# Zeroing the score banks on ScalarE, adding the residual on TensorE, and ending VectorE on its branch, in a decode step of an attention and MLP block

## The chip, the core and the metric

The kernel runs on one core of a Trainium2 chip. The metric is the device time of one execution in microseconds (us), lower is better. A core has five engines with queues of their own: TensorE (PE; its weight loads are listed as PEld), VectorE (DVE), ScalarE (ACT), GpSimd (POOL) and SyncE (SP), which here issues the DMA transfers. PSUM has eight banks of 128 x 512 fp32; matrix products land there.

## The reference

One token (`x`, 512 wide) goes through a grouped-query attention over a cache of 16,384 positions and then through an MLP, each with a layer norm ahead and a residual behind. There are 32 query heads, 8 key/value heads and a head width of 128.

```python
x = A_x
h = x + _A_ref(_layernorm(x), k_cache, v_cache, wq, wo)
h2 = h + _B_ref(_layernorm(h), w1, w2, w3, w4)

def _A_ref(x, k_cache, v_cache, wq, wo):
    q = (x @ wq)
    ...
    scores = einsum("bhqd,bhkd->bhqk", q, k) * (Dh ** -0.5)
    o = einsum("bhqk,bhkd->bhqd", softmax(scores), v)
    return o.reshape(B, Sq, Hq * Dh) @ wo

def _B_ref(x, w1, w2, w3, w4):
    ...
    x1 = x + hs
    h2 = _gelu(_layernorm(x1) @ w3) @ w4
    return x1 + h2
```

With a single position (S = 1) the shifted groups in `_B_ref` hold nothing but padding, so `hs` is zero, `x1 = x`, and `w1` and `w2` are never read. What must be read is 79.17 MB, nearly all of it the two caches.

## The kernel before

**Program.** The kernel describes operations to a small planner, `Program`. Each operation names its engine, what it reads and writes (`r`, `w`) and the PSUM banks it uses (`bank`). The planner derives semaphore waits from these. Operations of one engine run in the order of the text. `_run` writes an engine's operations out straight. `_vector` and `_tensor` write VectorE's and TensorE's, with branches: TensorE's program is a loop over the four pairs of key/value heads, with inner loops, and a straight part behind it. An operation whose function is `None` (L805 for VectorE, L808 for TensorE) marks the place of a conditional branch that is never taken and that carries a prefetch hint, placed at the program's start (L146, L223). VectorE's branch (L154) waits for the second piece of `w4` and has two instructions behind it: a wait for GpSimd's `xsum`, and the last addition (L815).

**Loads.** SyncE issues all large loads from `load` (L467), in program order: `wq`, then for each pair two halves of keys (4 MB each, into the two halves of `kb`) and the values (8 MB, into `vb`), then `wo` in three pieces, `w3` in two and `w4` in four, over the space of the keys. A load of keys waits until VectorE has transposed the half that it overwrites (L644); a load of values waits until TensorE has used the values before. The last pair's values come in two halves.

**A pair.** VectorE copies the pair's queries from `qb` into `qn` (L729). For each half `y`, VectorE transposes the keys piece by piece into `kt` (L644). TensorE first zeroes score bank `y` by a product of a zero column with itself (L655, part "clear"), since the 32 products of the half (L661, eight pieces of four, part "key") all add to that bank (`start=False`). In `_tensor` the clear has its own block, `pe_half`, with a wait of its own. Then comes the softmax: a maximum over both banks (L671), small steps, the exponential on ScalarE (L682), and two transposes of `p_sb` (L686). Meanwhile TensorE runs nine products that nobody reads (`unread`, L507, a loop of one product). Then come the sums, the values (L697, 64 products), and the gathering of the pair's output (L713 to L721).

**After the pairs.** ScalarE loads the table of the gelu (L746). `o_b` is multiplied by `wo` in 32 products (L766), of which the first 16 use the first piece, 12 the second and 4 the third; between the first 16 and the rest stand four unread products (L765). Then come the layer norm's sums (L521 to L533, L774), `hc` on ScalarE (L780), `w3` (L786, 16 products into bank 0), the inverse roots on VectorE and GpSimd (L540 to L569), `xs` and `xsum` on GpSimd (L793, L795; `xsum` is the sum of the two residuals), gelu (L798), a transpose to `hcol` (L802), and `w4`: 14 blocks `m` of four products (L810) that add in `n_ps`. Blocks 0 to 3 use w4's first piece, 4 to 8 its second, 9 to 12 its third, 13 its fourth. At the end VectorE adds `n_ps` and `xsum` into `fin` (L815), and SyncE writes four rows of `fin`, 256 bytes each, to the output (L817) and waits until they have arrived (L819).

Of the kernel before, what the change touches and what calls it, by code (L numbers as in the profile page):

```python
# [9 lines left out]
ALU = mybir.AluOpType  # L10
ACTF = mybir.ActivationFunctionType
# [13 lines left out]
class Program:  # L25
# [132 lines left out]
    def _tensor(self):  # L158
# [7 lines left out]
        last = pairs - 1  # L166

        def places(kind, *rest):
            return sorted(a for a in at if a[0] == kind and a[1:1 + len(rest)] == rest)
# [6 lines left out]
        def most(o):  # L176
            return max((d.val for d in o.deps if d.eng == "DVE" and not d.dma), default=0)
# [7 lines left out]
        for o in loop:  # L185
            if least(o) > have:
                have = least(o)
                if o.at[1] == last:
                    waits[o.at] = have
        first = waits["clear", last, 0, 0]  # L190
        keys = {("clear", last, 0, 0): first}
        keys |= {("key", last, y, c, 0): first + 1 + pieces * y + c for y in range(2) for c in range(pieces)}
        rest = {(a[0], a[-1]): v for a, v in waits.items() if a[0] in ("middle", "rest")}
        assert all(a in keys or (a[0], a[-1]) in rest for a in waits)
        waits |= keys | {("clear", last, 0, 0): first + 1}
        final = max(waits.values())


        have = 0
        for o in loop:  # L200
            a = o.at
            v = waits.get((a[0], last, *a[2:]))
            if v is not None:
                have = v + (a[1] - last) * step
                assert most(o) >= have - (a[0] == "clear")
            assert least(o) <= have


# [46 lines left out]

        nc.switch_bb("pe_queried", parent=None)
        eng.reg_add(rq, rq, width - 2 * width * pairs)
        eng.br_lt(rq, 2 * width - self.c0, "pe_query", "pe_half")

        nc.switch_bb("pe_half", parent=None)  # L260
        self.y = eng.snap(ry, donate=True, min_val=0, max_val=512)
        eng.wait_ge(vector, r)
        for a in places("clear", 1, 0):
            self._issue(eng, at[a])
        eng.br("pe_piece")

        nc.switch_bb("pe_piece", parent=None)
        self.q = eng.snap(rq, donate=True, min_val=0, max_val=QPAD)
        self.k = eng.snap(rk, donate=True, min_val=0, max_val=KP * (pieces - 1))
        eng.wait_ge(vector, r)  # L270
# [11 lines left out]
        eng.reg_add(ry, ry, 512)  # L282
        eng.reg_add(rq, rq, 4 * pieces)
        eng.reg_add(rk, rk, -KP * pieces)
        eng.br_lt(ry, 2 * 512, "pe_half", "pe_middle")

        nc.switch_bb("pe_middle", parent=None)
        now, again = first + 1 + 2 * pieces, 0
# [31 lines left out]
        eng.reg_add(r, r, first + 1 - (final - step))  # L320
        eng.reg_add(ry, ry, -2 * 512)
        eng.reg_add(rq, rq, -again)
        eng.br_lt(rl, v0 - 1 + parts * pairs, "pe_half", "pe_after")

        nc.switch_bb("pe_after", parent=None)
        seen[id(vector)] = final
# [14 lines left out]
            done = more + 1  # L341
        self._run(eng, ops[done:on], seen)

        eng.br_lt(rl, 0, "pe_half", "pe_on").branch_hint(hint)
        nc.switch_bb("pe_on", parent=None)
        self._run(eng, ops[on + 1:], seen)

# [28 lines left out]
def bass_sequential_preLN__gqa_block_cached__mixer_s_mlp__decode_kernel(  # L376
# [13 lines left out]
    with ExitStack() as ctx:  # L390
# [101 lines left out]
        def dve(fn, r=(), w=(), bank=()):  # L492
            return P.op("DVE", fn, r, w, bank)

        def act(fn, r=(), w=(), bank=()):
            return P.op("ACT", fn, r, w, bank)
# [4 lines left out]
        def pe(fn, r=(), w=(), bank=(), also=()):  # L501

            return P.op("PE", fn, r, w, bank, also=also)
# [6 lines left out]
        def piece(cuts, m):  # L510
            return [lo <= m < hi for lo, hi in cuts].index(True)

        def copies(col, n):

            return col.to_broadcast([col.shape[0], n])
# [132 lines left out]
            part = kt[:, :].rearrange("p (x f) -> p x f", x=2)[:, :, bass.ds(at, KP)]  # L648
            return part.rearrange("p x (l b s e) -> p b e x l s", l=8, b=2, s=32, e=2)[:, n // 2, n % 2, :, :, :]

        none = qn[:, 0, 0:1]

        def scores(j, y):
            P.part("clear", j, y)
            pe(lambda e: e.matmul(row[:, bass.ds(P.y, 512)], copies(none, 128), copies(none, 512),  # L655
                                  start=True, stop=False, skip_group_check=True),
               r=["qn"], w=[("s", y)], bank=[("s", y)])
            for c in range(8):
                P.part("key", j, y, c)
                for n in range(4):  # L660
                    pe(lambda e, n=n: e.matmul(  # L661
                        row[:, bass.ds(P.y, 512)], qn[:, n, bass.ds(P.q, 128)], key_piece(P.k, n),
                        start=False, stop=(n == 3), skip_group_check=True),
                       r=["qn", ("kt", c)], w=[("s", y)], bank=[("s", y)])

        both = dict(bank=[("s", 0), ("s", 1)])

        def softmax(j):

            s_all = s_ps[:, :, :].rearrange("p y f -> p (y f)")  # L670
            dve(lambda e: e.tensor_reduce(mx[:, :], s_all, AX.X, ALU.max), r=[("s", 0), ("s", 1)], w=["mx"], **both)  # L671
            dve(lambda e: e.tensor_scalar(mxd[:, :], ident_f[:, :], mx[:, 0:1], None, ALU.mult),  # L672
                r=["mx", "ident_f"], w=["mxd"])
            pe(lambda e: e.matmul(m_ps[:, 0:128], mean4[:, :], mxd[:, :], start=True, stop=True),  # L674
               r=["mxd", "mean4"], w=["m"], bank=["mn"])
            dve(lambda e: e.tensor_reduce(nm[:, :, :], m_ps[:, 0:128].rearrange("p (g n h) -> p g h n", g=2, h=REP),
                                          AX.X, ALU.min), r=["m"], w=["nm"], bank=["mn"])
            dve(lambda e: e.scalar_tensor_tensor(nmh[:, :], nm[:, :, :].rearrange("p g h -> p (g h)"),  # L678
                                                 32 * D * SCALE, maskgh[:, :, :].rearrange("p g h -> p (g h)"),
                                                 ALU.mult, ALU.mult, accum_out=bias[:, :]),  # L680
                r=["nm", "maskgh"], w=["nmh", "bias"])
            act(lambda e: e.activation(p_sb[:, :], s_all, ACTF.Exp, bias=bias[:, 0:1], scale=float(SCALE),  # L682
                                       accum_out=acc[:, :]),
                r=[("s", 0), ("s", 1), "bias"], w=["p", "acc"], **both)
            for g in range(2):
                dve(lambda e, g=g: e.transpose(pt[64 * g:64 * g + 64, :, :, g, :], p_sb[64 * g:64 * g + 64, :]),  # L686
                    r=["p"], w=["pt"])
# [37 lines left out]

        load_values(0)
        for j in range(PAIRS):
            P.part("query", j)
            dve(lambda e, j=j: e.tensor_copy(qn[:, :, :], qb[:, :, j, :]), r=["qb"], w=["qn"])  # L729
            for y in range(2):  # L730
                P.part("half", j, y)
                transpose_keys(y, (0, 2, 4, 6) if j < PAIRS - 1 else range(8) if y else (0, 1, 2, 4, 6))
                scores(j, y)
                if j < PAIRS - 1:
                    load_keys(j + 1, y)
            P.part("middle", j)
            softmax(j)
            unread(9)
            sums(j)
            values(j)  # L740
            P.part("rest", j)
            gather(j)
            if j < PAIRS - 1:
                load_values(j + 1)
# [16 lines left out]

        for r_ in range(32):
            q = r_ % 4
            if r_ == WO[1][0]:
                unread(4)  # L765
            pe(lambda e, r_=r_, q=q: e.matmul(O_ps[0][32 * q:32 * q + 32, :], copies(o_b[:, r_:r_ + 1], 32),  # L766
                                              wo_sb[:, r_ * D:(r_ + 1) * D], start=(r_ < 4), stop=(r_ >= 28)),
               r=["o_b"] + [("r", 0, n) for n in (piece(WO, r_),) if n], w=[("O", 0)], bank=[("O", 0)])
# [15 lines left out]
        for k in range(NCH):  # L784
            for q in range(4):
                pe(lambda e, k=k, q=q: e.matmul(s_ps[32 * q:32 * q + 32, 0, 0:FQ], hc[:, k, :],  # L786
                                                w3_sb[:, k, q * FQ:(q + 1) * FQ], start=(k == 0), stop=(k == NCH - 1)),
                   r=["hc"] + [("r", 1, n) for n in (piece(W3, k),) if n], w=[("s", 0)], bank=[("s", 0)])
        variances(1, (0, 1))
        seeds(1, (0, 1))  # L790
        inverse_root(1, 1, dve, act)
# [14 lines left out]
        for m in range(NHC):  # L806
            if m == W4[1][0]:
                pe(None)  # L808
            for o in range(4):
                pe(lambda e, m=m, o=o: e.matmul(  # L810
                    n_ps[32 * o:32 * o + 32, 0:128], hcol[:, m, :], w4_sb[:, m, o * 128:(o + 1) * 128],
                    start=(m == 0), stop=(m == NHC - 1),
                    skip_group_check=True),
                   r=[("hcol", 2 * m // NHC)] + [("r", 1, len(W3) + n) for n in (piece(W4, m),) if n], w=["n"], bank=["mn"])
        dve(lambda e: e.tensor_tensor(fin[:, :], n_ps[:, 0:128], xsum[:, :], ALU.add), r=["n", "xsum"], w=["fin"],  # L815
            bank=["mn"])
        P.op("SP", lambda e: e.dma_start(out[0, 0:1, :].rearrange("o (q j) -> (o q) j", q=4), fin[0:128:32, :]),  # L817
             r=["fin"], w=["out"], dma="out")
        P.op("SP", lambda e: e.nop(), r=["out"])  # L819
# [31 lines left out]
```

## Time and profile before

| | |
|---|---|
| median of three runs | 192.34 us (192.22 to 192.51) |
| time of the profiled execution | 192.24 us |
| its span, first to last instruction | 190.3 us |
| busy in the span: PE, DVE, ACT, POOL | 125.7, 117.9, 9.2, 7.4 us |
| moved by DMA | 79.20 MB, mean 416 GB/s |
| granted TensorE clock, mean | 0.86 |
| zeroing products, L655 | 8, together 4.0 us |
| exponentials on 128 x 1024, L682 | 4, 1.11 us each |
| last pair's second half of the values released by its load | 168.19 us |
| last addition, L815 | 187.32 us, 0.29 long |

All times inside a profile count from the start of the span. The span and the device time differ by what lies around the span, here 1.9 us. A line such as "L810 PE MATMUL banks<-kb,hcol" names the source line, the engine, the operation, what it writes and what it reads. In brackets stands how long the engine had been idle before it and what released it.

### The profile page before, as it was taken

The numbers are of one execution on the slowest core, as the hardware profiler recorded it, in microseconds if no ns is written. First come the engines' busy times: TensorE is split into PE (matmuls) and PEld (weight loads), VectorE is DVE, ScalarE is ACT, GpSimd is POOL, SyncE is SP. The second block draws the span as 40 slices with busy tenths as digits, with TensorE's granted clock in tenths as the row PEclk, the third lists the DMA queues.
The fourth block names the chain that finished last, engine by engine and source line by source line (L and its number), as shares of the span: only waits on it lengthen the run. The fifth ranks groups of instructions, "written<-read, shape, count | busy, mean of one in ns | idle before, by whom it ended". The sixth has DMA issues, their size and how long they took to land.

```text
span 190.3 us, 2315 instructions
## 1 busy us (share of the span) xinstructions
PE 125.7 (66%) x733; PEld 48.5 (25%) x733; DVE 117.9 (62%) x152; ACT 9.2 (5%) x16; POOL 7.4 (4%) x16
## 2 busy tenths in 40 slices
PE   0119709997770599964944989658359996865552
PEld 0103303442230233321311433213113332321131
DVE  6740799995523989845049989450479895522270
ACT  3000000000200000011000000020000000500030
POOL 7100000000000000000000000000000000000050
PEclk9999995899999579998585899996858999799755
DMA  6999999999999999997999999889999999999991
GB/s 221 441 441 441 441 441 441 441 441 441 399 413 420 420 551 441 441 441 331 441 441 441 551 399 399 386 379 420 441 441 441 441 441 441 441 386 395 423 408 46
DMA packets 3330, 79.20 MB, mean 416 GB/s; under 512 B 384, under 2 KB 512, under 8 KB 1280
## 3 DMA queue, kind: packets, MB, share of 16 engines
q1 hardware_dynamic: 3320, 79.17, 97.1%
q8 instruction: 1, 0.02, 0.0%
q14 instruction: 1, 0.01, 0.0%
q10 hardware_dynamic: 8, 0.00, 0.0%
HBM read 79.17 MB, written 0.00 MB: 416 GB/s over the span
## 4 chain that ended last, share of the span: by engine, by line
DMA 66%; DVE 15%; PE 14%; issue 2%; SPq 1%; DVEq 0%
DMA kb<-in_A_k_cache_dram 45%; DMA kb<-in_B_w_dram 14%; DVE kt L644 14%; PE banks L661 9%; DMA vb<-in_A_wq_dram 6%; PE banks L621 5%; SPq L467 1%; DVE qcol L628 1%; PE banks L655 1%; DVE qb L635 0%; PE banks L810 0%; DVE xn L612 0%; DVE fin L815 0%; SPq L139 0%; DVEq L139 0%
## 5 line engine op out<-in xcount | busy, mean ns | idle before, releaser
L644 DVE STREAM_TRANSPOSE kt<-kb 128x2048 int32<-128x2048 int32 (+1 forms) x37 | 71.3, 1989 | 6.9 <-DMA kb<-in_A_k_cache_dram 5.3
L661 PE MATMUL banks<-kt,qn 128*128 x256 | 68.9, 416 | 0.9 <-DVE kt L644 0.2
L661 PEld LDWEIGHTS banks<-kt,qn 128*128 x256 | 26.5, 104 | 41.4 <-issue 23.8
L697 PE MATMUL banks<-vb,pt 128*32 128x512 bf16 x256 | 19.2, 463 | 3.5 <-POOLq L482 3.0
L655 PE MATMUL banks<-qn 128*128 128x512 bf16 x8 | 4.0, 495 | 19.6 <-DVE kt L644 19.5
L713 DVE TENSOR_SCALAR od<-banks,rowc 128x128 f32<-128x128 f32 x4 | 1.4, 351 | 21.9 <-PE banks L697 21.9
L507 PE MATMUL banks<-qb 128*128 128x512 bf16 x40 | 14.3, 434 | 0.3
L686 DVE STREAM_TRANSPOSE pt<-p_sb 64x1024 bf16<-64x1024 bf16 x8 | 9.9, 1240 | 5.4 <-ACT p_sb L682 5.3
L621 PE MATMUL banks<-vb,xn 128*128 x32 | 9.0, 451 | 6.1 <-DVE xn L612 6.1
L682 ACT ACTIVATE p_sb<-banks,bias 128x1024 bf16<-128x1024 f32 x4 | 4.5, 1114 | 155.4 <-DVE nmh L678 155.4
L697 PEld LDWEIGHTS banks<-vb,pt 128*32 128x32 bf16 x256 | 7.6, 114 | 13.3 <-issue 5.6
L671 DVE TENSOR_REDUCE mx<-banks 128x1 f32<-128x1024 f32 x4 | 4.9, 1225 | 8.1 <-PE banks L661 8.1
L628 DVE STREAM_TRANSPOSE qcol<-banks 64x1024 f32<-64x1024 f32 x4 | 4.8, 1228 | 7.2 <-PE banks L621 7.2
L563 POOL TENSOR_SCALAR st<-st 128x1 f32<-128x1 f32 x1 | 0.2, 243 | 176.5 <-DVE st L543 176.5
L507 PEld LDWEIGHTS banks<-qb 128*128 128x128 bf16 x40 | 4.2, 107 | 9.3 <-issue 8.8
L655 PEld LDWEIGHTS banks<-qn 128*128 128x128 bf16 x8 | 0.8, 100 | 22.5 <-issue 22.3
L621 PEld LDWEIGHTS banks<-vb,xn 128*128 128x128 bf16 x32 | 3.6, 113 | 11.1 <-issue 8.6
L674 PE MATMUL banks<-mxd,mean 128*128 128x128 f32 x8 | 2.0, 332 | 6.6 <-DVE mxd L672 6.6
L719 PE MATMUL banks<-od,zo 128*32 128x128 f32 x8 | 1.6, 285 | 6.5 <-DVE od L716 6.5
L716 DVE SCALAR_TENSOR_TENSOR od<-banks,rowc,od 128x128 f32<-128x128 f32 x12 | 4.2, 351 | 0.4
L766 PE MATMUL banks<-kb,o_b 128*32 128x512 bf16 x32 | 2.5, 409 | 3.0 <-DMA kb<-in_A_wo_dram 1.8
L588 PE MATMUL banks<-x,quarter 4*128 4x128 bf16 x1 | 0.3, 285 | 6.0 <-DVE quarter L586 6.0
(77 smaller groups left out, 48.5 us busy)
## 6 DMA issues: line engine op xcount, KB each, us to landing
kb<-in_A_k_cache_dram SPq DMA_DIRECT2D x8, 4096.0 KB, 29.7
vb<-in_A_v_cache_dram SPq DMA_DIRECT2D x2, 4096.0 KB, 29.8
vb<-in_A_wq_dram SPq DMA_DIRECT2D x1, 4096.0 KB, 12.2
kb<-in_A_wo_dram SPq DMA_DIRECT2D x1, 2048.0 KB, 25.0
kb<-in_B_w_dram SPq DMA_DIRECT2D x2, 896.0 KB, 23.2
kb<-in_A_wo_dram SPq DMA_DIRECT2D x1, 1536.0 KB, 28.3
kb<-in_B_w_dram SPq DMA_DIRECT2D x2, 512.0 KB, 25.9
kb<-in_B_w_dram SPq DMA_DIRECT2D x1, 640.0 KB, 26.0
```

Source lines behind the costliest of these rows:

```text
L507: P.op("PE", lambda e: e.matmul(O_ps[1][:, :], field[:, 0:128], field[:, 0:512], start=True, stop=True), r=["qb"], bank=[("O", 1)], times= ...
L621: pe(lambda e, k=k: e.matmul(row[:, bass.ds(P.b + P.b0, 512)], copies(xn[:, k:k + 1], 128), wq_k[:, k, bass.ds(P.c + P.c0, REP * DH)], sta ...
L628: dve(lambda e, g=g, b=b, half=half: e.transpose(qcol[64 * g:64 * g + 64, 2 * b:2 * b + 2, :, :].rearrange("p e m u -> p (e m u)"), half.r ...
L644: P.op("DVE", lambda e, view=view: e.transpose(view(kt), view(kb[y])), r=[("r", y, i) for i in range(RPARTS)], w=[("kt", t + i) for i in r ...
L655: pe(lambda e: e.matmul(row[:, bass.ds(P.y, 512)], copies(none, 128), copies(none, 512), start=True, stop=False, skip_group_check=True), r ...
L661: pe(lambda e, n=n: e.matmul(row[:, bass.ds(P.y, 512)], qn[:, n, bass.ds(P.q, 128)], key_piece(P.k, n), start=False, stop=(n == 3), skip_g ...
L671: dve(lambda e: e.tensor_reduce(mx[:, :], s_all, AX.X, ALU.max), r=[("s", 0), ("s", 1)], w=["mx"], **both)
L682: act(lambda e: e.activation(p_sb[:, :], s_all, ACTF.Exp, bias=bias[:, 0:1], scale=float(SCALE), accum_out=acc[:, :]), r=[("s", 0), ("s", ...
L686: dve(lambda e, g=g: e.transpose(pt[64 * g:64 * g + 64, :, :, g, :], p_sb[64 * g:64 * g + 64, :]), r=["p"], w=["pt"])
L697: pe(lambda e, l=l, ct=ct, ch=ch: e.matmul(O_ps[0][32 * ct:32 * ct + 32, :], pt[:, l, ch, :, :].rearrange("p g u -> p (g u)"), tiles[:, l ...
L716: dve(lambda e, block=block, c=c: e.scalar_tensor_tensor(od[:, :], block, rowc[:, c:c + 1], od[:, :], ALU.mult, ALU.add), r=[key, "rowc", ...
L766: pe(lambda e, r_=r_, q=q: e.matmul(O_ps[0][32 * q:32 * q + 32, :], copies(o_b[:, r_:r_ + 1], 32), wo_sb[:, r_ * D:(r_ + 1) * D], start=(r ...
```

## The change

There are four parts.

1. The eight zeroing products leave TensorE, and with them the block `pe_half` and its wait. ScalarE writes zeros into both score banks in one pass of 128 x 1024 per pair, ahead of the pair's `qn`; the copy into `qn` now waits for it, and through it TensorE does.
2. The residual `xsum` is added by TensorE: one fp32 product of the identity with `xsum` into `n_ps`, ahead of block 9 of `w4`.
3. The last pass, from PSUM into `fin`, is then a plain copy and goes from VectorE to ScalarE. Nothing stands behind VectorE's branch any more.
4. The four unread products among the `wo` products go. Three unread products, in the same kind of loop, stand behind the `w3` products.

```diff
-        first = waits["clear", last, 0, 0]
-        keys = {("clear", last, 0, 0): first}
-        keys |= {("key", last, y, c, 0): first + 1 + pieces * y + c for y in range(2) for c in range(pieces)}
+        first = waits["key", last, 0, 0, 0] - 1
+        keys = {("key", last, y, c, 0): first + 1 + pieces * y + c for y in range(2) for c in range(pieces)}
...
-        nc.switch_bb("pe_half", parent=None)
+        eng.br_lt(rq, 2 * width - self.c0, "pe_query", "pe_piece")
+
+        nc.switch_bb("pe_piece", parent=None)
         self.y = eng.snap(ry, donate=True, min_val=0, max_val=512)
-        eng.wait_ge(vector, r)
-        for a in places("clear", 1, 0):
-            self._issue(eng, at[a])
-        eng.br("pe_piece")
...
-            P.part("clear", j, y)
-            pe(lambda e: e.matmul(row[:, bass.ds(P.y, 512)], copies(none, 128), copies(none, 512),
-                                  start=True, stop=False, skip_group_check=True),
-               r=["qn"], w=[("s", y)], bank=[("s", y)])
...
+        s_all = s_ps[:, :, :].rearrange("p y f -> p (y f)")
+
+        def clear():
+            act(lambda e: e.activation(s_all, copies(mean4[:, 0:1], 1024), ACTF.Identity, scale=0.0),
+                r=["mean4", "p"], w=[("s", 0), ("s", 1)], **both)
...
         for j in range(PAIRS):
+            P.part()
+            clear()
             P.part("query", j)
-            dve(lambda e, j=j: e.tensor_copy(qn[:, :, :], qb[:, :, j, :]), r=["qb"], w=["qn"])
+            dve(lambda e, j=j: e.tensor_copy(qn[:, :, :], qb[:, :, j, :]), r=["qb", ("s", 0), ("s", 1)], w=["qn"])
...
-            if r_ == WO[1][0]:
-                unread(4)
...
+        unread(3)
         variances(1, (0, 1))
...
+            if m == W4[2][0]:
+                pe(lambda e: e.matmul(n_ps[:, 0:128], ident_f[:, :], xsum[:, :], start=False, stop=False,
+                                      skip_group_check=True), r=["ident_f", "xsum"], w=["n"], bank=["mn"])
...
-        dve(lambda e: e.tensor_tensor(fin[:, :], n_ps[:, 0:128], xsum[:, :], ALU.add), r=["n", "xsum"], w=["fin"],
-            bank=["mn"])
+        act(lambda e: e.activation(fin[:, :], n_ps[:, 0:128], ACTF.Identity), r=["n"], w=["fin"], bank=["mn"])
```

## The prediction, made before the change was run

> **What bounds the kernel now.** I read the strip of DMA busy tenths and the table of queues first, then the chain of waits, then the last 10 us in the timeline, then the DMA queues of the last 2 us alone.
>
> ```profile
> DMA  6999999999999999997999999889999999999991
> q1 hardware_dynamic: 3320, 79.17, 97.1%
> q8 instruction: 1, 0.02, 0.0%
> q14 instruction: 1, 0.01, 0.0%
> DMA 66%; DVE 15%; PE 14%; issue 2%; SPq 1%; DVEq 0%
> kb<-in_A_k_cache_dram SPq DMA_DIRECT2D x8, 4096.0 KB, 29.7
> ```
>
> The 16 DMA engines work from the first slice to the last but one. A load of 4096 KB takes 9.7 us at this rate (whole loads arrive at 22.8, 32.5, 51.9, 61.6, 71.3 and so on, 9.7 apart and twice that for the values, which are twice as large), yet lands 29.7 us after its issue: it stands behind others. So no step of a pair sets the end; a load issued 1 us sooner only queues 1 us longer. What sets the end is 79.17 MB through a full queue, and what follows its last bytes. The end of the chain in order of time (start, length, what) and the timeline there:
>
> ```profile
> 159.67 26.82 DMA kb<-in_B_w_dram
> 186.50 0.04 issue
> 186.54 0.75 PE banks L810 x20
> 187.32 0.29 DVE fin L815
> ```
>
> ```profile
> 185.08 1.15 PE L810 MATMUL banks<-kb,hcol 128*32 128x128 bf16 x36 [1.29 <-DVE hcol L802]
> 185.42 0.46 POOL L795 TENSOR_TENSOR xsum<-hr,xs 128x128 f32<-128x128 f32 x1
> 186.54 0.72 PE L810 MATMUL banks<-kb,hcol 128*32 128x128 bf16 x20 [0.31 <-DMA kb<-in_B_w_dram]
> 187.64 0.62 SPq L817 DMA_DIRECT2D out_dram<-fin  x1
> ```
>
> Then the DMA answer for 188.5 to 190.3 us (40 slices of 0.045 us) and SyncE's last wait:
>
> ```profile
> DMA  0000000000400000000000000000000000000000
> GB/s 0 0 0 0 0 0 0 6 12 0 182 0 0 0 0 0 0 6 0 0 0 0 0 0 0 0 0 0 0 0 0 0 0 0 0 0 0 0 0 0
> q14 instruction: 1, 0.01, 1.1%
> q1 hardware_dynamic: 8, 0.00, 0.4%
> SPq L819 <- DMA out_dram<-fin: 2.1, 1, 2.1
> ```
>
> The output is four rows of 256 bytes. Three go at 188.82 to 188.91 (slices 7 and 8). Slice 10, 188.95 to 189.0, is an 8 KB instruction packet (182 GB/s x 0.045 us); the packet's own record is 188.97 to 189.28. Only then, in slice 17 (189.27), goes the fourth row: it starts as the packet ends, so it shared that DMA engine. The trace's records of arrivals on the output's semaphore put three rows at 189.24 to 189.25 and the fourth at 190.31; SyncE sees it at 190.33, and the span ends at 190.35. **The last 1.06 us are one row behind an instruction fetch.** Whose? It starts 1.36 us after VectorE's last instruction (187.32 + 0.29 = 187.61). ScalarE ended at 184.78, GpSimd at 185.88, TensorE at 187.27, and no 8 KB packet follows them by 1.4 us. So it goes with VectorE's end.
>
> **The change part by part**, against the profiled execution: span 190.35, time 192.24 (1.89 around the span); the median of the three, 192.34, is 0.10 above it.
>
> Zeroing. Eight products leave TensorE:
>
> ```profile
> L655 PE MATMUL banks<-qn 128*128 128x512 bf16 x8 | 4.0, 495 | 19.6 <-DVE kt L644 19.5
> ```
>
> 8 x 0.495 = 4.0 us, 1.2 of it on the chain; hidden by the queue in pairs 0 to 2: the least that stands ahead of a load at its issue is 9.7 us (the values' at 22.81, keys until 32.5), so loads issued sooner arrive no sooner. In pair 3 the second half of the values waits for its load (0.57 us idle, until 168.19), so nothing moves after it. ScalarE gets four 128x1024 passes. Nearest row: the exponential at L682, 1.11 us on the same two banks. It may run right behind the exponential of the pair before (50.2 to 51.3), while the copy into qn that now waits for it starts at 58.82; for pair 0 from 21.7 (banks 0 and 1 transposed out) to 22.8, against 26.06. Behind qn on VectorE stand the transposes of keys, on which the issue of loads depends: not late, with 3 us spare or more. Bounds: 1.0 us (0.20 of L561 below plus 1,023 x 0.775 ns) up to 3.7 with a table load of 1.28 before it and one before the exponential; the latter would push 165.70 to 167.0 and the values' end 170.1 to 170.7, which the wait for wo's second piece (1.39 idle before 176.72) takes up. Cost 0.
>
> Unread products. The four at 174.29 (1.04 us) go; TensorE then waits for wo until 176.72 anyway. If their absence lets the clock halve at 174.6 instead of 178.0, three rounds of L766 take 0.427 apiece (the spacing of L507 at half clock, 160.99 to 161.42) instead of 0.216: streaming ends at 178.0 against the last piece's 177.98. At most 0.05 late, into 0.5 us of slack (below). Three new ones follow w3's last round (183.20 + 0.37 = 183.57): 3 x 0.427 = 1.28, done streaming at 184.85, before hcol releases L810 at 185.08. Cost 0.
>
> ```profile
> 181.40:184.80 3.40, 1.70 (x17) 0.46 (x16) 2.41 (x12) 1.46 (x4) 2.10 (x7) 0.50 1.01 408
> ```
>
> They raise TensorE's busy time (the first number after the 3.40 of the stretch) from 1.70 to 2.98. Would that lift the clock of 0.50? From 27.85 to 31.26 it was 74% busy and stayed at 0.50; the next, full 3.4 us brought 1.00. I take 0.50. At 1.00, the four rounds ahead of the last piece take 0.22, not 0.43, and the last products end about 0.17 sooner. The Trainium skill (TensorE: Matmul & The Clock Gate, Part 1) wants one busy window of about 3.4 us on a free-running grid; this is just under one, so by it too the clock would mostly stay, and the sum is the same; where it opens, the time is 0.17 lower.
>
> Residual. Two fp32 passes go between m = 8 and m = 9. m = 8's last products start at 185.92; the next slot is 186.03. xsum is there at 185.88. Nearest rows at half clock: L774's passes start 0.216 apart, L531's, with a full weight load, 0.235. So 186.03 + 0.235 + 0.216 = 186.48, inside the gap before 186.54. Bounds: 0 to 0.2 late (L674 as a whole takes 0.54, plus a weight load of 0.15). I take 0, nearest to L531. Behind its wait for GpSimd stand m = 9 to 13 and with them the end, but that wait is over first.
>
> The last pass. DVE's 0.292 goes, and ScalarE reads the bank:
>
> ```profile
> L561 ACT ACTIVATE st<-st x1: 203/203/203, 182.2 to 182.2; 128x1 f32<-128x1 f32 x1
> L798 ACT ACTIVATE hg<-banks,st 128x224 bf16<-128x224 f32 x2 | 0.9, 490 | 1.6 <-DVE st L569 1.6
> ```
>
> From L798 to L682, (1114 - 490) / 800 = 0.78 ns an element; L561, like the new pass without a pointer operand, gives 0.20 + 127 x 0.78 ns = 0.30; L780 (128 wide, with a bias) 0.40 above, 0.29 below. I take 0.30: +0.01. Start after TensorE's end and SyncE's start after it (0.05 and 0.03) stay.
>
> VectorE's end. Its last act is then the branch at L154, 185.23 + 0.07 = 185.30 (it waits for w4's second piece, as before); the fetch 1.36 later falls at 186.66, after the last data (186.35) and 2.2 us ahead of the output rows. The fourth row then arrives with the three: -1.06, bounds 0 (another fetch takes its place) and -1.06; I take all of it, as the arrivals show it.
>
> Sum: 0 + 0 + 0 + 0.01 - 1.06 = **-1.05**: span 189.30, time 192.24 - 1.05 = **191.2** (by the median 191.3).
>
> **The rivals.** (a) *The fetch belongs to the end of whichever compute engine is last.* For: it follows the last one here too. Against: of three engines that end earlier none shows one, which this cannot explain only if each has its own. ScalarE, last now, would bring it at the same distance: +0.01 to +0.2, time 192.2 to 192.4, no change.
> (b) *Slower: VectorE's next fetch meets the row.* A second q14 packet of 8 KB starts at 191.66, 2.69 after the first. Moved along, it falls at 186.66 + 2.69 = 189.35. A row not yet arrived then waits to 189.66, and by before's 1.04 from packet to arrival ends at 190.70, span 190.74: +0.39, time 192.6. Rows arrive at 189.26 by my sum, so it decides from 0.1 us of lateness in the tail on, and the residual's bound is 0.2. Against: 191.66 also follows SyncE's end by 1.3 and may hang on that.
> (c) *Only the packet's lateness is saved*, 189.27 - 188.87 = 0.40, and the slow arrival has its own cause: 191.85.
> (d) *The moved loop's back jumps cost a fetch of code.* Against: L338's branch back took 0.22 us a round here and L323's over the whole loop of a pair 0.22. Price: the 16 KB packet on q8, about 1.1 us behind TensorE's branch and 1.4 long, 2.5 in all, less 0.23 + 0.5 of slack: 191.2 + 1.8 = 193.0. The Trainium skill (Runtime: NRT & Kernel Launch, Instruction fetch mechanics) states this rule: code is prefetched in sequence, and a taken branch outside the resident blocks stalls on a DMA. No run here shows such a stall.
>
> **How the numbers follow.** Forecast 0.62; (a) 0.12; (b) 0.15; (c) 0.06; (d) and the like 0.05. 0.2% (0.38 us) is about what can be told from no change. Faster: forecast and (c), 0.68; same: (a), 0.12; slower: (b) and (d), 0.20. The range reaches from the forecast with the open clock (191.0, less 0.1 of spread) over (c) and (a) to 192.5; (b) and (d) are left out. The forecast alone: 190.9 to 191.6.
>
> **What would show it.** Right: in the last 2 us all four rows in neighbouring slices with no q14 packet between; an 8 KB packet near 186.7; SyncE's last wait 1.0, not 2.1; ScalarE's fin of 0.30 starting near 187.32; last bytes near 186.5 as before; clock 0.50 at the end. Wrong: a q14 packet 1.36 behind ScalarE's end (a), or at 189.35 (b); an idle TensorE between L786 and L810 (d); L810's m = 9 starting after 186.6 (residual).

## The result, and the profile after

| | before | changed |
|---|---|---|
| median | 192.29 us (192.08 to 192.57, 22 executions) | 190.82 us (190.46 to 192.31, 22 executions) |
| profiled execution: time, span | 192.24, 190.35 | 190.78, 189.37 |
| time less span, mean over executions with a recorded span | 1.95 | 1.39 |
| last pass into `fin` starts | 187.32 | 187.40 |
| three rows of the output, and the fourth, have arrived | 189.26, 190.32 | 189.29, 189.34 |

The changed kernel is faster by 0.6%: ratio to before 0.9937 (95% interval 0.9921 to 0.9953). The forecast was 191.2. The trace shows the forecast movements, the packet's and the late row's. The gain is larger, and in the trace it has two parts, of which only one was forecast: a shorter span, and less time around the span. Of the 22 executions 14 lie at 190.46 to 190.99, 3 at 191.06 to 191.30, and 5 at 191.96 to 192.31. Those five matter below.

The tail in the timeline of the changed kernel (start, length, engine, line, tiles; line numbers are those of the changed kernel):

```profile
185.32 1.15 PE L804 MATMUL banks<-kb,hcol 128*32 128x128 bf16 x36
185.63 0.46 POOL L786 TENSOR_TENSOR xsum<-hr,xs 128x128 f32<-128x128 f32 x1
186.40 0.56 PE L801 MATMUL banks<-xsum,ident_f 128*128 128x128 f32 x2
186.89 0.46 PE L804 MATMUL banks<-kb,hcol 128*32 128x128 bf16 x20
187.40 0.28 ACT L809 ACTIVATE fin<-banks 128x128 bf16<-128x128 f32 x1 [2.41 <-PE banks L804]
187.71 0.62 SPq L810 DMA_DIRECT2D out_dram<-fin  x1
```

Up to the issue of the output nothing is gained: it comes at 187.71, 0.07 later than before. Then the DMA answer for 188.5 to 190.3, the same 40 slices as before, and SyncE's last wait:

```profile
DMA  0000000000000000000000070000000000000000
GB/s 0 0 0 0 0 0 0 0 0 11 12 0 0 0 0 0 0 0 0 0 0 0 0 182 0 0 0 0 0 0 0 0 0 0 0 0 0 0 0 0
q14 instruction: 1, 0.01, 1.9%
q1 hardware_dynamic: 8, 0.00, 0.4%
SPq L812 <- DMA out_dram<-fin: 1.0, 1, 1.0
```

All four rows lie in slices 9 and 10 (188.90 to 189.0). The 8 KB packet of q14 is now 0.55 behind them, in slice 23 (its record: 189.54 to 190.09), and SyncE's wait is 1.0 instead of 2.1. That packet is VectorE's second. The first is found earlier, between 186.3 and 187.8 (slices of 0.0375 us):

```profile
GB/s 55 55 27 27 27 464 0 0 0 0 0 0 0 0 0 0 0 218 0 0 0 0 0 0 0 0 0 0 0 0 0 0 0 0 0 0 0 0 0 0
q8 instruction: 1, 0.02, 4.8%
q14 instruction: 1, 0.01, 2.2%
```

Slice 5 is the 16 KB packet on q8, slice 17 (186.97) the 8 KB packet on q14, after the last data (186.54) and 2.0 ahead of the rows.

The other parts: the zeroing pass on ScalarE takes 1.03 us and runs where nothing waits for it; the two stretches of about 3.4 us at the end show TensorE busier than before in the first, and the clock at 0.50 and then 0.75 (columns: stretch, length, busy time of PE, PEld, DVE, ACT, POOL with counts, granted clock, DMA share, GB/s).

```profile
L656 ACT ACTIVATE banks<-mean 128x1024 f32<-128x1024 f32 x4 | 4.1, 1027 | 19.9 <-DVE qcol L620 19.8
```

```profile
181.40:184.80 3.40, 2.71 (x21) 0.87 (x20) 2.20 (x12) 1.26 (x4) 1.90 (x7) 0.50 1.01 408
184.80:188.30 3.50, 2.55 (x60) 1.53 (x58) 0.91 (x2) 0.47 (x2) 1.11 (x3) 0.75 0.40 149
```

### The profile page after: what moved, and what is told of

Read it like the earlier page. It is cut to its first block, busy times and chain, and to the rows that moved or that the text cites. A ratio compares the mean times of both kernels' runs of the same rounds, so it can differ in the third digit from the quotient of the medians.

```text
span 189.4 us, 2296 instructions
## 1 busy us (share of the span) xinstructions
PE 127.5 (67%) x726; PEld 48.1 (25%) x726; DVE 117.6 (62%) x151; ACT 13.6 (7%) x21; POOL 7.4 (4%) x16
## 4 chain that ended last, share of the span: by engine, by line
DMA 66%; DVE 15%; PE 14%; issue 3%; ACT 0%; SPq 0%; DVEq 0%
DMA kb<-in_A_k_cache_dram 44%; DMA kb<-in_A_wo_dram 15%; DVE kt L636 13%; DMA vb<-in_A_wq_dram 7%; PE banks L613 5%; PE banks L647 5%; PE banks L756 1%; PE banks L776 1%; PE banks L804 1%; PE banks L499 1%; DVE qcol L620 1%; PE banks L764 1%; DVE qb L627 0%; PE banks L523 0%; PE banks L801 0%
## 5 line engine op out<-in xcount | busy, mean ns | idle before, releaser
L647 PE MATMUL banks<-kt,qn 128*128 x256 | 69.9, 416 | 21.0 <-DVE kt L636 19.6
L687 PE MATMUL banks<-vb,pt 128*32 128x512 bf16 x256 | 20.8, 497 | 2.9 <-POOLq L474 2.9
L613 PE MATMUL banks<-vb,xn 128*128 x32 | 9.7, 479 | 6.3 <-DVE xn L604 6.3
L687 PEld LDWEIGHTS banks<-vb,pt 128*32 128x32 bf16 x256 | 8.3, 121 | 13.6 <-issue 7.6
L656 ACT ACTIVATE banks<-mean 128x1024 f32<-128x1024 f32 x4 | 4.1, 1027 | 19.9 <-DVE qcol L620 19.8
L694 PE MATMUL banks<-acc,zd 128*32 128x1 f32 x8 | 0.9, 180 | 5.0 <-DVE pt L676 5.0
```

Source lines behind the costliest of these rows:

```text
L613: pe(lambda e, k=k: e.matmul(row[:, bass.ds(P.b + P.b0, 512)], copies(xn[:, k:k + 1], 128), wq_k[:, k, bass.ds(P.c + P.c0, REP * DH)], sta ...
L647: pe(lambda e, n=n: e.matmul(row[:, bass.ds(P.y, 512)], qn[:, n, bass.ds(P.q, 128)], key_piece(P.k, n), start=False, stop=(n == 3), skip_g ...
L656: act(lambda e: e.activation(s_all, copies(mean4[:, 0:1], 1024), ACTF.Identity, scale=0.0), r=["mean4", "p"], w=[("s", 0), ("s", 1)], **both)
L687: pe(lambda e, l=l, ct=ct, ch=ch: e.matmul(O_ps[0][32 * ct:32 * ct + 32, :], pt[:, l, ch, :, :].rearrange("p g u -> p (g u)"), tiles[:, l ...
```

## The experiments

Three theories. The **fetch theory**: an 8 KB instruction packet goes with VectorE's end, and a row of the output that meets it arrives late. The **last-engine theory**, rival (a) of the prediction: the packet goes with whichever compute engine ends last. The **work theory**: the gain comes from work taken off TensorE and VectorE. Beside them stands rival (b), VectorE's second packet. Twelve kernels were run.

### One part at a time

`end_only` is the kernel before with parts 2 and 3:

```diff
+            if m == W4[2][0]:
+                pe(lambda e: e.matmul(n_ps[:, 0:128], ident_f[:, :], xsum[:, :], start=False, stop=False,
+                                      skip_group_check=True), r=["ident_f", "xsum"], w=["n"], bank=["mn"])
...
-        dve(lambda e: e.tensor_tensor(fin[:, :], n_ps[:, 0:128], xsum[:, :], ALU.add), ...
+        act(lambda e: e.activation(fin[:, :], n_ps[:, 0:128], ACTF.Identity), r=["n"], w=["fin"], bank=["mn"])
```

> The kernel before with parts 2 and 3 alone (residual on TensorE, last pass on ScalarE, nothing behind VectorE's branch); the zeroing and the four unread products stay. Fetch theory (an 8 KB instruction packet on q14 follows VectorE's own end by about 1.4 us, and the output row that meets it costs 1.06 us): the whole gain is here, 0.9 to 1.1 us faster than before, four rows in neighbouring slices, SyncE's last wait 1.0 instead of 2.1. Since the clock will be 0.50 at the end and the residual's two passes start late (186.40 in the changed kernel), the tail is 0.2 to 0.4 later than in the changed kernel, so some executions may meet VectorE's second packet and show 192.2 to 192.6. Work theory (the gain comes from the products taken off TensorE and their unread replacement): no gain, 192.2 to 192.6 in all executions, and a q14 packet is no matter.

Measured: 190.88 us (190.82 to 190.91), ratio to before 0.9923 (0.9908 to 0.9938). The whole gain is here. Its last pass starts 0.20 later than in the changed kernel, its rows arrive at 189.50 and 189.54, and the second packet starts at 189.57, only just behind them.

`zero_only` is the kernel before with part 1 (`clear()` on ScalarE, the `clear` products gone, the rest as before).

> The kernel before with part 1 alone (score banks zeroed by ScalarE). Fetch theory: within 0.2% of before, 192.1 to 192.5, since the DMA queue hides it; the q14 packet still falls between the third and the fourth row, SyncE's last wait 2.1. Work theory: 0.5 to 1.4 us faster, since 4 us of products leave TensorE.

Measured: 192.23 us (192.03 to 192.42), ratio 0.9997 (0.9988 to 1.0006). The DMA answer for 188.5 to 190.3 shows the row behind the packet again (slice 13 the packet, slice 20 the row):

```profile
GB/s 0 0 0 0 0 0 0 0 0 0 0 17 0 182 0 0 0 0 0 0 6 0 0 0 0 0 0 0 0 0 0 0 0 0 0 0 0 0 0 0
SPq L811 <- DMA out_dram<-fin: 2.1, 1, 2.1
```

So 4.0 us of products less on TensorE, 1.2 of them on the chain of waits, are worth nothing behind a full DMA queue.

`loop_only` is the kernel before with part 4:

```diff
-            if r_ == WO[1][0]:
-                unread(4)
...
+        unread(3)
         variances(1, (0, 1))
```

> The kernel before with part 4 alone: the four unread products go from the products of wo, three go ahead of w4. VectorE still ends with the last addition. Fetch theory: within 0.3 us of before (a row still meets the packet, since both follow the last addition), 192.0 to 192.4. Work theory: a part of the gain, 191.0 to 191.8.

Measured: 192.10 us (192.04 to 192.49), ratio 0.9997 (0.9988 to 1.0006). Nothing measurable.

### VectorE's end moved back

`copy_on_vector` is the changed kernel with the last pass, the plain copy, on VectorE:

```diff
-        act(lambda e: e.activation(fin[:, :], n_ps[:, 0:128], ACTF.Identity), r=["n"], w=["fin"], bank=["mn"])
+        dve(lambda e: e.tensor_copy(fin[:, :], n_ps[:, 0:128]), r=["n"], w=["fin"], bank=["mn"])
```

> The changed kernel with its last pass (a plain copy) on VectorE, behind its branch, all else as changed. Fetch theory, now with its second half (the time around the span is 1.3 to 1.5 us where VectorE ends at its branch by 185.5, 1.8 to 2.2 where it ends later): a q14 packet 1.6 after the copy's start, a row 1.0 late, and the time around the span back at 1.9: 191.9 to 192.5, the whole gain gone. Work theory: the gain stays, 190.5 to 191.0.

Measured: 192.49 us (191.94 to 193.07), ratio 1.0012 (0.9999 to 1.0024). The gain is gone with this one instruction, at the same length, though its last pass also starts 0.16 later than in the changed kernel:

```profile
187.56 0.29 DVE L809 CAST fin<-banks 128x128 bf16<-128x128 f32 x1 [1.85 <-PE banks L804]
187.88 0.63 SPq L810 DMA_DIRECT2D out_dram<-fin  x1
```

```profile
GB/s 0 0 0 0 0 0 0 0 0 0 182 0 0 11 6 0 0 0 0 0 0 0 0 0 6 0 0 0 0 0 0 0 0 0 0 0 0 0 0 0
SPq L812 <- DMA out_dram<-fin: 2.1, 1, 2.1
```

The work theory is out. To tell the fetch theory from the last-engine theory, the next two leave the last pass on ScalarE and give VectorE something to do that nobody waits for. `tail_work` has two products:

```diff
         dve(None, r=[("r", 1, len(W3) + 1)])
+        for key, t in (("xs", xs), ("od", od)):
+            dve(lambda e, t=t: e.scalar_tensor_tensor(t[:, :], hr[:, :], 1.0, hr[:, :], ALU.mult, ALU.mult),
+                r=["hr", ("r", 1, len(W3) + 3)], w=[key])
```

> The changed kernel with two 128x128 products of hr with itself on VectorE behind its branch, waiting for w4's last piece and read by nobody: VectorE then ends near 187.6 instead of 185.47, and nothing waits for it. Fetch theory: the q14 packet moves to 188.9 to 189.1, a row arrives 0.7 to 1.1 us late, and the time goes back to 191.8 to 192.3 in nearly all executions. Last-engine theory (the packet goes with whichever compute engine ends last) and work theory: no change from the changed kernel, 190.5 to 191.0.

Measured: 191.74 us (191.60 to 191.98), ratio 0.9971 (0.9959 to 0.9983). `tail_more` has four (into `hx` and `osum` too).

> The changed kernel with four products of hr with itself on VectorE behind its branch, read by nobody (two before): VectorE ends at about 187.75 and its first packet falls at 188.85 to 189.1, on the rows. Fetch theory: a row is written 0.3 to 0.4 late and arrives 1.0 late, 191.9 to 192.6, more than with two products (191.74). Last-engine theory and work theory: as the changed kernel, 190.5 to 191.0.

Measured: 191.55 us (191.41 to 191.59), ratio 0.9959 (0.9945 to 0.9972). Against the changed kernel's 190.82 both lose 0.7 to 0.9 us by work that is on nobody's path; against its median on `tail_more`'s own chip (191.22, `after_again` below) `tail_more` loses 0.3. In `tail_work` 0.16 of the loss is the last pass, which starts at 187.56; in `tail_more` it starts as early as ever, at 187.32. `tail_work` speaks against the last-engine theory: as in the changed kernel ScalarE ends last (187.84, VectorE 187.35), yet the first packet comes at 188.47 instead of 186.97. `tail_more` can't tell the two theories apart, since there VectorE itself ends last:

```profile
187.32 0.28 ACT L812 ACTIVATE fin<-banks 128x128 bf16<-128x128 f32 x1 [2.43 <-PE banks L807]
187.49 0.28 DVE L798 SCALAR_TENSOR_TENSOR osum<-hr 128x128 f32<-128x128 f32 x1
```

But the expectation of where the packet falls was wrong. In `tail_more` VectorE ends at 187.77 and the packet comes at 188.14, only 0.37 behind; in `tail_work` 187.35 and 188.47. Nor did four products cost more than two. What fits is the moment at which VectorE's last wait is over (186.86 and 186.87), not the end of the work behind it: see the table below.

### VectorE's end put later

`late_branch` is the changed kernel with VectorE's branch waiting for w4's third piece, which puts the rows between the two packets:

```diff
-        dve(None, r=[("r", 1, len(W3) + 1)])
+        dve(None, r=[("r", 1, len(W3) + 2)])
```

> The changed kernel with VectorE's branch waiting for w4's third piece (186.6) instead of its second (185.4): VectorE ends near 186.75. Fetch theory with rival (b), by which the executions near 192.2 of the changed kernel (5 of 22) are those where the second q14 packet meets a row: the first packet falls at 188.1 to 188.3, the second at 190.7 or later, both clear of the rows at 188.9 to 189.3, so the executions near 192 vanish and all lie at 190.4 to 191.0. If the executions near 192 have another cause (clock, arrival of the data), they stay, about one in four. Work theory: no change from the changed kernel.

Measured: 191.65 us (191.41 to 191.65), ratio 0.9959 (0.9945 to 0.9972). The packets fell as expected (188.21 and 190.70), no row was late and no execution came near 192; yet the time rose by 0.8. Two things were missed. Its clock stayed at 0.50 to the end, and the last pass started at 187.87. And the time around the span went from 1.39 to 1.94.

```profile
184.80:188.30 3.50, 2.53 (x58) 1.84 (x58) 0.90 (x2) 0.45 (x2) 1.01 (x3) 0.50 0.42 156
187.87 0.28 ACT L809 ACTIVATE fin<-banks 128x128 bf16<-128x128 f32 x1 [2.89 <-PE banks L804]
SPq L812 <- DMA out_dram<-fin: 1.0, 1, 1.0
```

`tiled_late` is the same with the residual in four products (below).

> The residual in four products and VectorE's branch waiting for w4's third piece. Packets of VectorE at 188.1 to 188.3 and from 190.6 on, rows at 188.8 to 189.2: by the fetch theory no row is late in any execution, all lie at 190.3 to 191.0. If a packet 0.6 us ahead of the rows still delays a row's arrival (as the single profile with work behind the branch hints: packet 188.47, rows written at 189.1, one arrival at 189.82 instead of 189.49), some show 0.3 to 0.4 more, 191.0 to 191.4.

Measured: 191.84 us (191.54 to 192.04), ratio 0.9974 (0.9964 to 0.9984): worse than with the early branch. The packet ends at 188.62, the rows are written from 188.70 on, and one of them arrives at 189.61, 0.49 behind the others.

What the profiles show together, in us (the packets from the trace's records of DMA packets, the arrivals from those of the output's semaphore; VectorE's last wait is that of its branch where nothing stands behind the branch; the last column is the mean over a kernel's executions with a recorded span):

| kernel | VectorE's last wait over | q14 packets start | rows written: three, fourth | arrived: three, fourth | time less span |
|---|---|---|---|---|---|
| before | 187.32 | 188.97, 191.66 | 188.88, 189.27 | 189.26, 190.32 | 1.95 |
| `zero_only` | 187.46 | 189.12, 191.56 | 189.04, 189.42 | 189.41, 190.47 | 1.96 |
| `loop_only` | 187.29 | 188.72, 191.17 | 188.86, 189.20 | 189.24, 190.07 | 1.93 |
| `copy_on_vector` | 187.56 | 188.99, 191.70 | 189.13, 189.60 | 189.49, 190.60 | 1.96 |
| `tail_work` | 186.86 | 188.47, 191.07 | 189.12, 189.15 | 189.49, 189.82 | 1.97 |
| `tail_more` | 186.87 | 188.14, 190.85 | 188.87, 188.90 | 189.26, 189.49 | 1.91 |
| `late_branch` | 186.67 | 188.21, 190.70 | 189.42, 189.46 | 189.76, 189.80 | 1.94 |
| `tiled_late` | 186.57 | 188.13, 190.71 | 188.73, 188.82 | 189.12, 189.61 | 2.14 |
| changed | 185.41 | 186.97, 189.54 | 188.95, 188.98 | 189.29, 189.34 | 1.39 |
| `end_only` | 185.42 | 187.02, 189.57 | 189.16, 189.19 | 189.50, 189.54 | 1.35 |
| `tiled_residual` | 185.17 | 186.72, 189.28 | 188.64, 188.67 | 188.98, 189.02 | 1.57 |
| `tiled_noloop` | 185.18 | 186.73, 189.23 | 188.81, 188.84 | 189.15, 189.19 | 1.34 |

Three things stand in it. The first packet starts 1.27 to 1.66 after VectorE's last wait is over, whatever the other engines do, and the second 2.43 to 2.71 after the first. Where a packet runs at about the time at which the fourth row is due (0.03 behind the third), that row is written only as the packet ends, 0.3 to 0.5 behind the others, and arrives 0.8 to 1.1 behind them; the other three aren't late, even where they are written during the packet (`loop_only`, 188.86 within 188.72 to 189.21). A fourth row written 0.2 to 0.4 after the packet's end still arrives 0.2 to 0.5 late; with 0.8 between them (`late_branch`) it is on time. And the time around the span has two levels: 1.91 to 2.14 where the last wait is over at 186.6 or later, 1.34 to 1.57 where it is over by 185.5.

### VectorE's second packet

`after_again` is the changed kernel, once more, for a comparison on one chip.

> The changed kernel itself, beside the next three on one chip, for its own spread: 190.4 to 191.0 in most executions. By rival (b) an execution whose end comes late (clock 0.50 to the end, last pass from about 187.6 on) writes its rows at 189.2 to 189.5 and meets VectorE's second packet at 189.5: 191.9 to 192.4, and nothing between 191.1 and 191.9 unless the end is late without the meeting.

Measured: 191.22 us in the median of 11, ratio 0.9952 (0.9934 to 0.9970): two at 190.42 and 190.79, six at 191.11 to 191.33, three at 192.05 to 192.21. The group in the middle was not expected. `delayed_end` forces the meeting of rival (b): two more passes of ScalarE into tiles nobody reads put the rows where the second packet falls.

```diff
+        act(lambda e: e.activation(od[:, :], n_ps[:, 0:128], ACTF.Identity), r=["n"], w=["od"], bank=["mn"])
+        act(lambda e: e.activation(osum[:, 0:128], n_ps[:, 0:128], ACTF.Identity), r=["n"], w=["osum2"], bank=["mn"])
         act(lambda e: e.activation(fin[:, :], n_ps[:, 0:128], ACTF.Identity), r=["n"], w=["fin"], bank=["mn"])
```

> The changed kernel with two more passes of ScalarE over the same 128x128 of the bank, into tiles nobody reads, ahead of the last pass. Rows are written 0.4 to 0.5 later, at 189.3 to 189.5, beside VectorE's second packet at 189.5. By rival (b) a row is then late by 0.5 to 1.0 in most executions: 191.7 to 192.4, time around the span still 1.3 to 1.5. Without (b): 0.4 to 0.5 more than the changed kernel and no more, 190.9 to 191.7.

Measured: 192.06 us in the median of 12, ratio 0.9972 (0.9952 to 0.9993): four at 190.76 to 191.12, eight at 192.03 to 192.59, nothing between. The profile is of the upper group:

```profile
188.01 0.28 ACT L811 ACTIVATE fin<-banks 128x128 bf16<-128x128 f32 x1
188.32 0.63 SPq L812 DMA_DIRECT2D out_dram<-fin  x1
```

```profile
GB/s 0 0 0 0 0 0 0 0 0 0 0 0 0 0 0 0 0 0 0 182 0 0 0 17 0 0 0 0 0 0 6 0 0 0 0 0 0 0 0 0
SPq L814 <- DMA out_dram<-fin: 1.8, 1, 1.8
```

In this answer for 188.5 to 190.3 slice 19 is VectorE's second packet (189.38 to 189.86), slice 23 three rows, slice 30 the fourth. It arrives at 190.72, 0.76 behind the others. The time around the span is 1.34, as in the changed kernel. So the mechanism of rival (b) is shown in this trace. That the five executions of 22 at 191.96 to 192.31 are such meetings fits their spans (190.6 to 191.0 against 189.1 to 189.7) and their time around the span (1.31 to 1.43), but none of those has been seen in a trace by itself. What makes the group at 191.1 to 191.3 stays open.

### The residual's place in the tail

`tiled_residual` is the changed kernel with the residual as four products:

```diff
-                pe(lambda e: e.matmul(n_ps[:, 0:128], ident_f[:, :], xsum[:, :], start=False, stop=False,
-                                      skip_group_check=True), r=["ident_f", "xsum"], w=["n"], bank=["mn"])
+                for o in range(4):
+                    pe(lambda e, o=o: e.matmul(n_ps[32 * o:32 * o + 32, 0:128], ident_f[:, 32 * o:32 * o + 32], xsum[:, :],
+                                               start=False, stop=False, skip_group_check=True),
+                       r=["ident_f", "xsum"], w=["n"], bank=["mn"])
```

> The changed kernel with the residual as four products of 32 columns of the identity, one for each group of 32 output rows, as the products of w4 around it are, instead of one over all 128. In the changed kernel its weight load starts 0.24 behind block 8's last start and block 9 follows 0.73 after that at clock 0.50. If this is a change between products of the whole array and of its quarters, the four products pass in 0.45 to 0.5 and block 9 starts at its data (186.5 to 186.7) instead of 187.1: 0.2 to 0.5 us faster than the changed kernel where the clock is 0.50, 0 to 0.2 elsewhere, and fewer executions near 192. If it is two fp32 passes as such, no change.

Measured: 190.82 us (190.55 to 191.05), ratio 0.9923 (0.9910 to 0.9936), beside 191.22 (190.42 to 192.21) for the changed kernel on the same chip. No execution of six is beyond 191.05. `tiled_noloop` leaves the three unread products out as well (`unread(3)` gone).

> The residual in four products, and no unread products ahead of w4. If the loop opens the clock for the last products in some executions (stretches of 3.4 us that it fills), the clock stays at 0.50 to the end in all, the last pass starts 0.1 to 0.3 later than with the loop and the time is 190.7 to 191.3. If the loop does nothing, the same as with the loop, 190.55 to 191.05.

Measured: 190.67 us (190.54 to 190.88), ratio 0.9920 (0.9908 to 0.9933). The loop isn't needed for the time. The tail of `tiled_noloop`, and of `end_only` with the residual as one product, both at clock 0.50:

```profile
185.93 0.29 PEld L801 LDWEIGHTS banks<-xsum,ident_f 128*32 128x32 f32 x8
186.03 0.64 PE L801 MATMUL banks<-xsum,ident_f 128*32 128x128 f32 x8
186.48 0.46 PEld L805 LDWEIGHTS banks<-kb,hcol 128*32 128x32 bf16 x20 [0.26 <-DMA kb<-in_B_w_dram]
187.26 0.28 ACT L810 ACTIVATE fin<-banks 128x128 bf16<-128x128 f32 x1 [2.47 <-PE banks L805]
```

```profile
186.09 0.50 PEld L810 LDWEIGHTS banks<-xsum,ident_f 128*128 128x128 f32 x2 [0.20 <-issue]
186.09 0.80 PE L810 MATMUL banks<-xsum,ident_f 128*128 128x128 f32 x2
186.82 0.46 PEld L813 LDWEIGHTS banks<-kb,hcol 128*32 128x32 bf16 x20 [0.23 <-DMA kb<-in_B_w_dram]
187.60 0.28 ACT L818 ACTIVATE fin<-banks 128x128 bf16<-128x128 f32 x1 [3.19 <-PE banks L813]
```

The four products stand between block 8 and block 9 without a gap, and block 9 starts 0.05 after its data (arrived 186.43). The one product starts after 0.20 us in which TensorE waited for nothing that the profile shows, and block 9 follows its start by 0.73; here that is 0.14 after its data (arrived 186.68).

## Why the prediction was right, and where it was wrong

**The signs** that the prediction named came, all but the clock: VectorE ends on its branch, its packet moves to 186.97 (forecast 186.66), the fourth row arrives with the others, SyncE's last wait is 1.0 instead of 2.1. The term of -1.06 measured -1.01 in the profile (the fourth row 0.05 behind the third instead of 1.06). `end_only` and `copy_on_vector` show that VectorE's early end makes the gain, and no other part.

**"1.89 around the span"** is the step that failed. The sum took it as fixed; in the profiled execution it falls to 1.41, and that alone is more than the 0.4 by which the forecast was short. It goes with VectorE's end in all twelve kernels of the table. Why isn't shown, since the trace's instructions end with the span. The packets hint at it: where VectorE's last wait is late, its second packet ends 1.39 to 1.64 after the span, and where it is early, at most 0.72 after. In `delayed_end` it ends 0.89 before the span does, and the time around the span is no less, 1.34. So it may be that an execution lasts until VectorE's second packet is in, and never less than about 1.3 beyond the span; this wasn't tried.

**Two accounts of the gain** are left by this. If the late row and the time around the span simply add up, the row was worth 1.0 and the rest 0.5, and the prediction's mechanism is right. If the execution lasts until the second packet is in, the late row cost the kernel before nothing, since it had arrived long before that packet ended (190.32 against 191.97), and the term of -1.06 was near the truth by luck. `late_branch`, with no late row, is still 0.8 above the changed kernel, part of it by its later last pass; that fits both. No run has a late VectorE, an early last pass and all rows on time, which would tell them apart. Where VectorE ends early, the late row does cost the time: `delayed_end`, 192.03 to 192.59 against 190.76 to 191.12.

**The residual**, "I take 0, nearest to L531", was mis-sized, and the sign that the prediction gave for it came: block 9 starts at 186.89, past 186.6. At clock 0.50 block 9's weight load follows the residual's by 0.73, not 0.45, and in `late_branch` starts 0.45 after its data (187.09 against the arrival at 186.64). Of the nearest rows, L774's stood among products of their own shape and L531's alone behind a wait; here products of the whole array stand between products of 32 columns. The Trainium skill (TensorEngine Tiling (Array Packing), Key Properties) states that changing the tiling mode drains TensorE; the gap of 0.20 before the residual and the four products without one agree with it. That the drain is the whole of the difference isn't shown: the one product's weight loads are also longer (0.29 to 0.34 in `late_branch`, 0.17 to 0.18 for the four in `tiled_noloop`).

**The clock**, "I take 0.50", was wrong for the profiled execution and right for others. It opened at 186.57, ahead of block 9, and pulled in the last 20 products (0.46 instead of 0.72), so that the late block 9 cost only 0.08 at the last pass. In `late_branch` it stayed at 0.50. In these traces it opens and closes in stretches of 3.41 us or a multiple that lie differently against the span in each profiled execution (it opened at 186.57 here, at 187.17 in `tail_work`, at 185.56 in `tiled_residual`). The Trainium skill (TensorE: Matmul & The Clock Gate, Part 1) states that the clock's window is free-running, and these stretches agree with it. Where the clock opens may be what spreads the tail from execution to execution; only the profiled executions show where the clock opened.

**The zeroing, the unread products and ScalarE's pass** were costed at 0, 0 and +0.01: `zero_only` and `loop_only` both 0.9997, and the pass 0.28 us where 0.30 was worked out.

**The rivals.** (a) is out by the packet at 186.97 in the changed kernel and by `tail_work`. (b) is real, but, if the upper group is it, in a part of the executions only, at 191.96 to 192.31 instead of 192.6: in `delayed_end` the row arrives 0.86 after the packet's end rather than 1.04, and the time around the span is smaller. Its condition was lateness in the tail, and the late residual gives some; with the residual in four products no execution of 11 came near 192, against 8 of 33 of the changed kernel. (c) and (d) were not seen. The statement "it goes with VectorE's end" needs one correction: it goes with the end of VectorE's last wait; work queued behind that doesn't push the packet out.

## What to carry to other kernels

When a kernel is bound by its DMA queue, look at what follows the last byte: which engine still has instructions behind its last wait, and whether an instruction packet runs on the DMA engines while the output is written. Moving one pass to another engine was worth 0.7% here, while 4 us of TensorE work taken away were worth nothing. A single product of another array shape in a run of products at the end cost 0.73 here where its passes come to 0.45; try it in the shape of its neighbours.

## What the runs showed of the hardware

An 8 KB instruction packet of 0.3 to 0.6 us delayed the fourth output row's arrival by 0.8 to 1.1 us where the two met, and by 0.2 to 0.5 us where the row was written 0.2 to 0.4 us after it. The Trainium skill (Runtime: NRT & Kernel Launch, Instruction fetch mechanics) calls the cost of crossing from one 16 KiB block of instructions to the next mostly hidden; at the end of these kernels the packets were not hidden (`delayed_end`). The time around the span, which I had taken for a constant, is 0.5 us shorter when VectorE is done with its last wait 1.1 us earlier or more (185.5 against 186.6 and later).
